# Two GpSimd drains among the last passes of a fused recurrence and mixture-of-experts kernel

## The chip, the cores and the metric

The kernel runs on one core of one Trainium2 chip. Its time is device microseconds of one launch, and the median of several runs counts. A core has five engines that run their own instruction queues: TensorE (PE in the profile; PEld is its weight load), VectorE (DVE), ScalarE (ACT), GpSimd (POOL) and SyncE (SP), which here issues transfers alone. They meet through semaphores.

## The reference

The first half is a gated linear recurrence over 768 steps in 4 x 8 heads of 48 channels; the second sends each of the 3072 resulting rows (8 heads x 48 = 384 wide) to one of 16 experts.

```python
f = 1.0 / (1.0 + np.exp(-f_logit))
for t in range(S):
    state = f[:, :, t, :, None] * state + np.einsum('bhd,bhe->bhde', k[:, :, t], v[:, :, t])
    y[:, :, t] = np.einsum('bhd,bhde->bhe', q[:, :, t], state)
# x: y with the heads of one step side by side, (3072, 384)
g_idx = argmax(x @ w_group);  e_idx = argmax(x @ w_expert[g_idx])
h = np.maximum(x[tok] @ w1[g, e], 0.0)            # (rows, 1024)
out[tok] = (g_w * e_w)[:, None] * (h @ w2[g, e])  # (rows, 384)
```

`g_w` and `e_w` are the softmax weights of the chosen group and expert.

## The kernel before, in words

The recurrence is computed in chunks of 128 steps with matmuls, and its rows are written to a table in DRAM, `x_dram`, each with its weight and its row number behind it. Along the way the kernel works out which rows each expert gets, ranks the experts by their number of rows, and fixes its passes. Two experts have 128 of their rows done in two early passes beside the recurrence (`early`, line 492). Then come sixteen passes, numbered 0 to 15, with one expert in each: the first and the last are 128 rows wide, and the fourteen between have widths from 230 down to 174 rows, listed in `WIDTHS`. What is beyond these widths would go through a loop behind a test at line 997 (`more > 0`); with these inputs that branch isn't taken.

The passes go through `for n in range(GE - 1)` (line 887) and a last part behind it. A pass does the following.

- `fetch` (line 390) gathers its rows from `x_dram` into the tile `xg`, one indirect transfer for each block of up to 128 rows. GpSimd issues it.
- The rows are turned so that the features lie on partitions (`square_in`, or `turn_in` for 128 rows).
- `up` (line 434) multiplies by the first weights, and `down` (line 467) by the second. A narrow pass (`down_rows`) has its result with the rows on partitions at once; a wide pass has it turned, in `yT`.
- The wide result is turned back: on VectorE in 32 x 32 squares (`square_out`, line 419), one turn of the loop later, or, for the last wide pass, on TensorE (`turn_out`, line 485).
- `put` (line 445) scales each row by its weight into a tile `yt`, of which there are four in turn, and GpSimd scatters it by row number to the output with an indirect transfer.

GpSimd computes nothing in this half. It issues the gathers three passes ahead and the scatters, two for each wide pass. The functions on the path of a scatter are `scaled` (line 480), which the loop calls for the pass before the current one, and `turn_out`, which the last part calls for the pass before the last.

The order of TensorE, VectorE, ScalarE and SyncE is written out by hand (`tc.manual_schedule`, line 85). GpSimd isn't in that list; its instructions are placed by the scheduler. The weights come on SyncE's queue, three passes ahead.

At the end of the program the compiler puts a closing part that the profile shows under line 1046: every engine drains, they meet at a barrier, the semaphores are cleared, and they meet once more. A drain is an instruction of an engine's queue behind which nothing of this queue starts until the engine has finished what was before it.

Of the kernel before, what the change touches and what calls it, by code (L numbers as in the profile page):

```python
# [1 line left out]

# [1 line left out]

# [13 lines left out]
ET = mybir.EngineType  # L18
P = 128
# [4 lines left out]
def kernel(  # L24
# [12 lines left out]
    nc = tc.nc  # L37
    B, H, S, D = q.shape
    N, DM = out.shape
# [3 lines left out]
    GE = G * EG  # L43
# [4 lines left out]
    KO = DM // P  # L48
# [28 lines left out]
    def const(shape, dtype, name):  # L77
        return cp.tile(shape, dtype, tag=name, name=name)

    def bank(shape, name):  # L80
        return ps.tile(shape, FP32, tag="bank", name=name)
# [9 lines left out]
    ident = const([P, P], FP32, "ident")  # L91
# [294 lines left out]
    def load_weights(pool, ap):  # L386
        e = value(ap, GE - 1)
        return load_layer(pool, e, 1), load_layer(pool, e, 2)

    def fetch(pool, rows, n, top=N, late=False):  # L390

        w = {"n": n, "pool": pool, "early": top < N, "late": late, "blocks": [(j, min(P, n - j * P)) for j in range((n + P - 1) // P)]}
        w["x"] = pool.tile([P, len(w["blocks"]), RW], FP32, tag="xg", bufs=2 if pool is ep else 6, name="xg")
        for j, m in w["blocks"]:
            nc.gpsimd.indirect_dma_start(out=w["x"][:, j, :], out_offset=None, in_=x_dram[0:1 + top, :], in_offset=bass.IndirectOffsetOnAxis(ap=rows[:, j:j + 1], axis=0))  # L395
        return w
# [15 lines left out]
    def square_in(w):  # L412

        w["xT"] = room(w, KO, "xe")
        x = w["x"][:, :, 0:DM].rearrange("p j (o g c) -> p j g o c", o=KO, c=SQ)
        xT = w["xT_full"].rearrange("p o (j k c) -> p j k o c", j=2, c=SQ)
        squares(w, lambda n, k_, rk, g, rg: nc.vector.transpose(out=xT[rg, 0:n, k_], in_=x[rk, 0:n, g]))  # L417

    def square_out(w):

        w["rows"] = w["pool"].tile([P, 2, DM], FP32, tag="yr", name="yr")
        y = w["rows"].rearrange("p j (o g c) -> p j g o c", o=KO, c=SQ)
        yT = w["yT_full"].rearrange("p o (j k c) -> p j k o c", j=2, c=SQ)
        squares(w, lambda n, k_, rk, g, rg: nc.vector.transpose(out=y[rk, 0:n, g], in_=yT[rg, 0:n, k_]))  # L424

    def turn_in(w):
        w["xT"] = room(w, KO, "xe")
        for j, m in w["blocks"]:
            pt = bank([P, KO, P], "xg_ps")
            for ko in range(KO):  # L430
                nc.tensor.transpose(out=pt[:, ko, 0:m], in_=w["x"][0:m, j, ko * P:(ko + 1) * P], identity=ident[0:m, 0:m])
            (nc.scalar.copy if w["early"] else nc.vector.tensor_copy)(w["xT"][:, :, j * P:j * P + m], pt[:, :, 0:m])
# [12 lines left out]
    def put(w, j, m, yp):  # L445

        y = w["pool"].tile([P, DM], FP32, tag="yt", bufs=2 if w["pool"] is ep else 4, name="yt")
        if w["n"] == P or "rows" in w:
            nc.scalar.activation(y[0:m], yp[0:m], AF.Copy, scale=w["x"][0:m, j, DM:DM + 1])  # L449
        else:  # L450
            nc.vector.tensor_scalar(y[0:m], yp[0:m], w["x"][0:m, j, DM:DM + 1], None, OP.mult)
        sent = nc.gpsimd.indirect_dma_start(out=out, out_offset=bass.IndirectOffsetOnAxis(ap=w["x"][0:m, j, DM + 1:RW].bitcast(U32), axis=0), in_=y[0:m], in_offset=None, bounds_check=N - 1, oob_is_err=False)  # L452
        if not w["late"]:

            tc.declare_no_dep(sent.ins, group="outputs", reason="each pass has rows of its own")
            tc.add_to_no_dep_group("outputs", sent.ins)
# [10 lines left out]
    def down(w, w2):  # L467
        n = w["n"]
        if n == P:
            for _ in down_rows(w, w2):  # L470
                pass
            return
        w["yT"] = w["yT_full"][:, :, 0:n]
        for m in range(KO):
            yp = bank([P, n], "yo")
            for fo in range(FO):
                nc.tensor.matmul(yp, lhsT=w2[:, fo, m * P:(m + 1) * P], rhs=w["h"][:, fo, :], start=(fo == 0), stop=(fo == FO - 1))  # L477
            nc.scalar.copy(w["yT"][:, m, :], yp)  # L478

    def scaled(w):  # L480
        if w["n"] > P:
            for j, m in w["blocks"]:
                put(w, j, m, w["rows"][:, j, :])

    def turn_out(w):
        for j, m in w["blocks"]:
            pt = bank([P, DM], "y_ps")
            for k_ in range(KO):
                nc.tensor.transpose(out=pt[0:m, k_ * P:(k_ + 1) * P], in_=w["yT"][:, k_, j * P:j * P + m], identity=ident)
            put(w, j, m, pt)  # L490

    def early():

# [342 lines left out]
    def pass_of(n):  # L836
        p = PLACES[n]
        if p < EARLY:
            return fetch(mo, rows_p[:, p, 1:2], P)
        return fetch(mo, rows_p[:, p, :], WIDTHS[p - EARLY])  # L840
# [3 lines left out]
    def weakest():  # L844

        worst = const([P, 1], FP32, "worst")
        nc.vector.tensor_reduce(out=worst, in_=decays.rearrange("p c a n -> p (c a n)"), axis=AX, op=OP.min)
        wt = bank([1, P], "wt")
        nc.tensor.transpose(out=wt, in_=worst, identity=ident)
        far = const([1, 2], FP32, "far")  # L850
        nc.vector.tensor_reduce(out=far[:, 0:1], in_=wt, axis=AX, op=OP.min)
        nc.vector.tensor_scalar(far[:, 1:2], far[:, 0:1], math.exp(-SAFE), None, OP.is_lt)
        nc.vector.tensor_copy(fari, far[:, 1:2])

    def flags():

        nc.vector.tensor_copy(both[:, 0:1], fari)
        nc.vector.tensor_scalar(rest, b_end, 0, None, OP.is_gt)
        nc.vector.tensor_tensor(both[:, 1:2], fari, rest, OP.max)
# [13 lines left out]
    def run_up(n):  # L873
        for _ in up(ws[n], ahead[n][0]):
            pass
# [11 lines left out]
    for n in range(GE - 1):  # L887
        w = ws[n]
        if n + 3 < GE:
            ws[n + 3] = pass_of(n + 3)  # L890
        if n == 0:
            ahead[2] = load_weights(wp, who[0:1, PLACES[2]:PLACES[2] + 1])
        past, coming = ws.pop(n - 1, None), ws.get(n + 2)
        if past and past["n"] > P:
            square_out(past)
        if coming and coming["n"] > P:
            square_in(coming)
        if n + 2 < GE:
            run_up(n + 1)
        if past:  # L900
            scaled(past)
        if coming and coming["n"] == P:
            turn_in(coming)
        w["yT_full"] = outs[n % 2]
        down(w, ahead.pop(n)[1])
        if n + 3 < GE:
            ahead[n + 3] = load_weights(wq if n % 3 == 1 else wp, who[0:1, PLACES[n + 3]:PLACES[n + 3] + 1])
        if n == 2:
            with tc.tile_pool(name="tb", bufs=1) as tb:
                beyond(False, tb)  # L910
        if n == 3:
            weakest()
            flags()


    last_up = up(ws[GE - 1], ahead[GE - 1][0])
    next(last_up)
    turn_out(ws.pop(GE - 2))
    for _ in last_up:
        pass  # L920
# [76 lines left out]
    with tc.If(more > 0), ExitStack() as late:  # L997
# [5 lines left out]
        with tc.For_i(0, last, 1) as i:  # L1003
# [14 lines left out]
            w = fetch(ep, row, P, late=True)  # L1018
# [32 lines left out]
```

## Time and profile before

| | |
|---|---|
| time, median of 3 runs | 430.03 us (428.63 to 430.20) |
| span of the profiled execution | 427.1 us |
| busy: TensorE, VectorE, ScalarE, GpSimd | 408.0, 267.1, 157.0, 83.1 us |
| transfers in all | 88.98 MB, 208 GB/s over the span |
| on GpSimd's queue (q0) | 5792 packets, 11.92 MB |
| scatters on GpSimd (line 452) | 32, 1076 ns each to issue |
| gathers on GpSimd (line 395) | 30 and 2, 987 and 1022 ns each to issue |
| the last scatter starts | 416.39 us |

The span runs from the program's first to its last instruction and is a little shorter than the time of a run. Busy time counts what an engine computes [...]. A drain or a semaphore step counts as no busy time, though it has a duration; it stands in the views of one source line, marked with a q behind the engine's name. The release of a wait is worked out from semaphore events.

### The profile page before, as it was taken

How to read it: one execution, taken by the hardware profiler on the slowest of the kernel's cores; microseconds unless marked ns; L12 is line 12 of the kernel's file. 1: busy time of each engine (PE TensorE's matmuls, PEld its weight loads, DVE VectorE, ACT ScalarE, POOL GpSimd, SP SyncE). 2: the span in 40 equal slices, each digit the busy share in tenths (PEclk: the TensorE clock that was granted, in tenths of full speed). 3: DMA queues.
4: the chain of work that ended last, by engine and by line, in shares of the span. 5: the costliest groups of instructions: out<-in, count | busy, mean ns of one | idle time of the engine just before them, and what ended most of it. 6: DMA issues, size and time to landing. Idle time of an engine off the chain costs nothing.

```text
span 427.1 us, 10087 instructions
## 1 busy us (share of the span) xinstructions
PE 408.0 (96%) x4067; PEld 382.7 (90%) x4067; DVE 267.1 (63%) x778; ACT 157.0 (37%) x341; POOL 83.1 (19%) x127
## 2 busy tenths in 40 slices
PE   4999999999999999999999999999999999999990
PEld 2888989999889978989999999999999999999960
DVE  5665686868798741640899759468568559553410
ACT  5667666666664411211212123123123123123210
POOL 4000010101012047001042122221321321022120
PEclk9999999999999999999999999999999999999996
DMA  9999999999999639975828549569478569544010
GB/s 166 176 181 185 185 161 181 153 151 152 202 344 401 244 119 355 385 280 189 286 74 316 186 185 326 162 235 315 136 268 278 183 260 329 177 168 161 20 40 15
DMA packets 132121, 88.98 MB, mean 208 GB/s; under 512 B 102630, under 2 KB 122700, under 8 KB 132066
## 3 DMA queue, kind: packets, MB, share of 16 engines
q1 hardware_dynamic: 125666, 75.50, 65.8%
q0 software_dynamic: 5792, 11.92, 9.2%
q8 instruction: 34, 0.56, 0.6%
q10 hardware_dynamic: 608, 0.83, 0.6%
q14 instruction: 21, 0.17, 0.1%
HBM read 78.71 MB, written 9.83 MB: 207 GB/s over the span
## 4 chain that ended last, share of the span: by engine, by line
PE 49%; issue 30%; DMA 9%; POOL 6%; DVE 2%; ACT 2%; POOLq 0%; DVEq 0%
PE hp L441 12%; PE yo L477 6%; DMA out_dram<-yt,xg 6%; PE ap L645 4%; PE y L689 4%; POOL out_dram L452 4%; PE cs L585 4%; PE yo L462 4%; PE x_ps L729 3%; PE lT L704 2%; POOL xg L395 2%; PE tr_q L619 2%; DMA ends<-eq 2%; PE tr_k L619 2%; PE y L684 2%
## 5 line engine op out<-in xcount | busy, mean ns | idle before, releaser
L441 PE MATMUL hp<-xe,w 128*128 128x128 f32 (+14 forms) x864 | 138.6, 320 | 0.0
L441 PEld LDWEIGHTS hp<-xe,w 128*128 128x128 f32 x864 | 135.8, 190 | 0.8
L477 PE MATMUL yo<-h,w 128*128 128x230 f32 (+13 forms) x672 | 115.8, 333 | 0.0
L424 DVE STREAM_TRANSPOSE yr<-yT 32x192 f32<-32x192 f32 (+1 forms) x208 | 70.5, 339 | 70.4 <-ACT yT L478 67.8
L477 PEld LDWEIGHTS yo<-h,w 128*128 128x128 f32 x672 | 113.7, 190 | 0.2
L417 DVE STREAM_TRANSPOSE xe<-xg 32x192 f32<-32x192 f32 (+1 forms) x208 | 69.7, 335 | 8.6 <-PE hp L441 5.6
L442 ACT ACTIVATE h<-hp 128x256 f32<-128x256 f32 (+14 forms) x72 | 34.4, 478 | 103.6 <-PE hp L441 103.6
L452 POOL DMA_INDIRECT out_dram<-yt,xg x32 | 34.4, 1076 | 150.6 <-ACT yt L449 145.0
L478 ACT COPY yT<-yo 128x230 f32<-128x230 f32 (+13 forms) x42 | 13.5, 326 | 80.5 <-PE yo L477 80.5
L648 DVE TENSOR_TENSOR am<-ap,tri 128x512 f32<-128x512 f32 x48 | 29.8, 682 | 17.0 <-PE ap L645 16.9
L395 POOL DMA_INDIRECT xg<-x_dram,rows_p x30 | 29.6, 987 | 51.3 <-DMA out_dram<-yt,xg 27.5
L585 PE MATMUL cs<-ld_f,tri 128*128 128x384 f32 x48 | 19.5, 531 | 5.5 <-ACT ld_f L579 5.5
L645 PE MATMUL ap<-Tq,Tk 48*64 48x128 f32 x768 | 23.8, 272 | 0.2 <-ACT Tk L620 0.2
L689 PE MATMUL y<-am,v 128*64 128x128 f32 x384 | 23.3, 273 | 0.0
L645 PEld LDWEIGHTS ap<-Tq,Tk 48*64 48x64 f32 x768 | 20.8, 133 | 2.0 <-issue 1.1
L689 PEld LDWEIGHTS y<-am,v 128*64 128x64 f32 x384 | 21.5, 137 | 0.6 <-DVE am L648 0.5
L462 PE MATMUL yo<-w,h 128*128 128x384 f32 x64 | 21.3, 486 | 0.0
L462 PEld LDWEIGHTS yo<-w,h 128*128 128x128 f32 x64 | 11.9, 190 | 7.4
L585 PEld LDWEIGHTS cs<-ld_f,tri 128*128 128x128 f32 x48 | 8.5, 200 | 9.8 <-POOL blank L170 5.2
L592 POOL DMA_DIRECT2D ends<-eq x10 | 5.4, 541 | 60.3 <-ACT eq L586 60.3
L449 ACT ACTIVATE yt<-yr,xg 128x384 f32<-128x384 f32 (+13 forms) x26 | 14.4, 604 | 5.4 <-DVE yr L424 5.4
L692 ACT COPY xT<-y 128x512 f32<-128x512 f32 x24 | 12.9, 589 | 9.3 <-PE y L689 9.3
(170 smaller groups left out, 385.0 us busy)
## 6 DMA issues: line engine op xcount, KB each, us to landing
w<-in_moe_w_dram SPq DMA_DIRECT2D x34, 1536.0 KB, 10.2
qh<-in_q_dram SPq DMA_DIRECT2D x12, 384.0 KB, 6.8
ld_k<-in_k_dram SPq DMA_DIRECT2D x12, 384.0 KB, 6.5
v<-in_v_dram SPq DMA_DIRECT2D x12, 384.0 KB, 7.3
ld_f<-in_f_logit_dram SPq DMA_DIRECT2D x11, 384.0 KB, 6.6
x_dram<-x_kept SPq DMA_DIRECT2D x2, 1536.0 KB, 12.0
x_dram<-x POOLq DMA_DIRECT2D x2, 384.0 KB, 7.9
x_dram<-x ACTq DMA_DIRECT2D x2, 384.0 KB, 7.5
```

Of the source, the lines that this page charges most:

```text
L395: nc.gpsimd.indirect_dma_start(out=w["x"][:, j, :], out_offset=None, in_=x_dram[0:1 + top, :], in_offset=bass.IndirectOffsetOnAxis(ap=rows ...
L417: squares(w, lambda n, k_, rk, g, rg: nc.vector.transpose(out=xT[rg, 0:n, k_], in_=x[rk, 0:n, g]))
L424: squares(w, lambda n, k_, rk, g, rg: nc.vector.transpose(out=y[rk, 0:n, g], in_=yT[rg, 0:n, k_]))
L441: nc.tensor.matmul(hp[:, o, :], lhsT=w1[:, ko, (f + o) * P:(f + o + 1) * P], rhs=w["xT"][:, ko, :], start=(ko == 0), stop=(ko == KO - 1))
L442: nc.scalar.activation(h[:, f:f + 2, :], hp, AF.Relu)
L452: sent = nc.gpsimd.indirect_dma_start(out=out, out_offset=bass.IndirectOffsetOnAxis(ap=w["x"][0:m, j, DM + 1:RW].bitcast(U32), axis=0), in ...
L462: nc.tensor.matmul(yp, lhsT=w["h"][:, fo, :], rhs=w2[:, fo, :], start=(fo == 0), stop=(fo == FO - 1))
L477: nc.tensor.matmul(yp, lhsT=w2[:, fo, m * P:(m + 1) * P], rhs=w["h"][:, fo, :], start=(fo == 0), stop=(fo == FO - 1))
L585: nc.tensor.matmul(cs.rearrange("t h d -> t (h d)"), lhsT=tri, rhs=nl[:, b], start=True, stop=True)
L645: nc.tensor.matmul(ap[r][half, a, :], lhsT=w["Tk"][rows, b, a, half], rhs=w["Tq"][rows, b, a, :], start=True, stop=True)
L648: nc.vector.tensor_tensor(am[:, r], ap[r], tri.unsqueeze(1).broadcast_to((P, HP, P)), OP.mult)
L689: nc.tensor.matmul(ys[r][DP * b:DP * b + DP, a, :], lhsT=w["v"][:, b, 2 * a + r, :], rhs=w["am"][b][:, r, a, :], start=(c == 0 and a == 0) ...
```

## The change

Two drains are put into GpSimd's queue. The first comes behind the second scatter of pass 12 (the pass before the loop's current one when `n == GE - 3`), the second behind the second scatter of pass 14, which `turn_out` makes. A context manager `settled` does it: where it is switched on, GpSimd's instructions in its body keep their written order, and a `drain` follows them. It is on for a block `j` above 0, so for the second of two blocks alone. What they are for: GpSimd is to be done with the transfers it has issued so far at these two places, rather than at the end of the program.

```diff
-    def scaled(w):
+    def scaled(w, settle=False):
         if w["n"] > P:
             for j, m in w["blocks"]:
-                put(w, j, m, w["rows"][:, j, :])
+                with settled(settle and j):
+                    put(w, j, m, w["rows"][:, j, :])
+
+    @contextmanager
+    def settled(on):
+
+        with ExitStack() as turn:
+            if on:
+                turn.enter_context(tc.manual_schedule(engines={ET.Pool}))
+            yield
+            if on:
+                nc.gpsimd.drain()
 
     def turn_out(w):
         for j, m in w["blocks"]:
-            pt = bank([P, DM], "y_ps")
-            ...
-            put(w, j, m, pt)
+            with settled(j):
+                turn_out_block(w, j, m)
+
+    def turn_out_block(w, j, m):
+        pt = bank([P, DM], "y_ps")
+        ...
+        put(w, j, m, pt)
...
         if past:
-            scaled(past)
+
+            scaled(past, n == GE - 3)
```

No other instruction is added or taken away, and the order of the others is the same on each engine.

More of the change, by code (lines that the diff above doesn't have):

```diff
@@ L1 @@
-from contextlib import ExitStack
+from contextlib import ExitStack, contextmanager
 import math
@@ L478, in down @@
             nc.scalar.copy(w["yT"][:, m, :], yp)
-    def scaled(w):
+    def scaled(w, settle=False):
         if w["n"] > P:
             for j, m in w["blocks"]:
-                put(w, j, m, w["rows"][:, j, :])
+                with settled(settle and j):
[8 more added lines that the diff above has]
+                nc.gpsimd.drain()
     def turn_out(w):
         for j, m in w["blocks"]:
-            pt = bank([P, DM], "y_ps")
-            for k_ in range(KO):
-                nc.tensor.transpose(out=pt[0:m, k_ * P:(k_ + 1) * P], in_=w["yT"][:, k_, j * P:j * P + m], identity=ident)
-            put(w, j, m, pt)
+            with settled(j):
+                turn_out_block(w, j, m)
+    def turn_out_block(w, j, m):
+        pt = bank([P, DM], "y_ps")
+        for k_ in range(KO):
+            nc.tensor.transpose(out=pt[0:m, k_ * P:(k_ + 1) * P], in_=w["yT"][:, k_, j * P:j * P + m], identity=ident)
+        put(w, j, m, pt)
     def early():
```

## The prediction

> **What bounds the kernel now.** I read the whole page first, then the end of the span by windows, then GpSimd's own queue in order of time, and last the two lines of the program that hold its opening and its closing.
>
> The page says that the kernel is TensorE's for nearly all of its length: matmuls cover 96% of the span, and their row of tenths falls only in the last slice. The change touches no TensorE, VectorE or ScalarE instruction, so it can pay only where TensorE isn't at work: at the end.
>
> ```profile
> span 427.1 us, 10087 instructions
> PE 408.0 (96%) x4067; PEld 382.7 (90%) x4067; DVE 267.1 (63%) x778; ACT 157.0 (37%) x341; POOL 83.1 (19%) x127
> PE   4999999999999999999999999999999999999990
> DMA  9999999999999639975828549569478569544010
> ```
>
> The windows of the last 34 us are the view that carries the forecast. Columns: the window, its length, busy us (and instructions) of PE, PEld, DVE, ACT, POOL, then the clock and the DMA share and rate.
>
> ```profile
> 393.30:403.70 10.40, 10.40 (x72) 10.40 (x71) 5.12 (x16) 1.29 (x4) 0.01 (x1) 1.00 0.04 9
> 403.70:409.40 5.70, 5.70 (x52) 5.68 (x52) 1.13 (x2) 2.19 (x7) 4.12 (x4) 1.00 0.22 83
> 409.40:416.20 6.80, 6.05 (x24) 3.58 (x23) 0.00 (x0) 0.97 (x2) 0.00 (x0) 1.00 0.06 15
> 416.20:419.20 3.00, 0.00 (x0) 0.00 (x0) 0.00 (x0) 0.00 (x0) 0.99 (x1) 0.96 0.13 51
> 419.20:427.10 7.90, 0.00 (x0) 0.00 (x0) 0.00 (x0) 0.00 (x0) 0.00 (x0) 0.50 0.00 1
> ```
>
> In the last 7.9 us no engine computes and the DMA share is 0.00. What fills them is seen in the program's closing line (1046), GpSimd's part and SyncE's part of it; the opening line (1037) gives a drain that has nothing to drain. Columns: shortest/median/longest in ns, then first and last start in us.
>
> ```profile
> L1046 POOLq DRAIN  x3: 46/103/6767, 419.2 to 426.8; - x3
> L1046 POOLq EVENT_SEMAPHORE  x4: 17/17/17, 426.3 to 427.0; - x4
> ...
> L1046 SPq DRAIN  x3: 7/7/13, 419.9 to 426.6; - x3
> ...
> L1037 POOLq DRAIN  x1: 184/184/184, 0.3 to 0.3; - x1
> ```
>
> The first of GpSimd's three closing drains is the 6767 ns one (the next GpSimd record on the line, a semaphore step, comes at 426.3, and 419.2 + 6.77 is 426.0). All others wait for it: SyncE starts its own closing drains at 419.9, is at the barrier by 420.0, and sits there. So 6.8 us of the span are one GpSimd instruction on the path that sets the end.
>
> What does it drain? The last scatter starts at 416.39 and lands 2.5 us later, at 418.9, before this drain starts; so it waits for no data. It is bookkeeping, and the candidates for what it counts are the transfers that GpSimd has issued. Its queue near the end (start us, duration us, instruction, and in brackets the idle time before it):
>
> ```profile
> 390.74 1.00 POOL L452 DMA_INDIRECT out_dram<-yt,xg  x1 [11.63 <-ACT yt L449]
> 392.05 1.26 POOL L452 DMA_INDIRECT out_dram<-yt,xg  x1 [0.30 <-issue]
> 403.92 0.99 POOL L452 DMA_INDIRECT out_dram<-yt,xg  x1 [10.61 <-ACT yt L449]
> 405.21 0.96 POOL L452 DMA_INDIRECT out_dram<-yt,xg  x1 [0.30 <-issue]
> 406.88 1.00 POOL L452 DMA_INDIRECT out_dram<-yt,xg  x1 [0.71 <-DVE yt L451]
> 408.18 1.18 POOL L452 DMA_INDIRECT out_dram<-yt,xg  x1 [0.30 <-issue]
> 416.39 0.99 POOL L452 DMA_INDIRECT out_dram<-yt,xg  x1 [7.04 <-ACT yt L449]
> ```
>
> Between these pairs it idles 10.6 and 7.0 us. The issue counts are 32 scatters, 30 + 2 gathers, 10 of ends, 6 of meta and 2 of x: 82 transfers.
>
> **What the skill says.** The Trainium skill, "VectorE: DVE Perf Modes", section "The DRAIN you can't avoid", puts the drains of a program's opening and closing at about 12 ns on all engines. The trace agrees for four engines (SyncE 7 to 13 ns) and contradicts it for GpSimd: 46, 103, 184 and 6767 ns. "Perfetto Trace Analysis", section "Sequencer-only Instruction (DRAIN, etc)", says that the profiler shows execution alone for such an instruction and not its semaphore wait; so 6.77 us would be the drain's own work, which fits the landing above. "DMA: Bandwidth & Descriptors", section "SWDGE vs HWDGE vs iDMA", says that two GpSimd cores write a pair of descriptors per operation into rings in SBUF. That makes a ledger that grows with each transfer plausible, but no page states what a GpSimd drain costs. "PSUM — Partial Sum Buffer", section "Engine vs sequencer instructions", says a drain waits for the engine to go fully idle; whether that takes in transfers in flight no run here shows yet, so I price both readings.
>
> **The change part by part.** The only new instructions are two GpSimd drains: one after the second scatter of pass 12 (392.05), one after the second of pass 14 (408.18). The order hints around them leave every instruction on all five engines in its old order, so they cost nothing; splitting the function that turns rows out costs nothing for the same reason.
>
> *Price of a drain.* A bare one takes 46, 103 or 184 ns; I take 0.11 us, about their mean. If the rest of the last drain is shared by the 82 transfers, each costs (6.77 - 0.11) / 82 = 0.081 us. That is my estimate from this trace; the trace holds no second loaded drain to test it. The bounds: 0 per transfer (all 6.77 fixed), or 0.081 per transfer.
>
> *Drain 1* has 82 - 5 = 77 transfers behind it: 0.11 + 77 x 0.081 = 6.3 us. Scatter 392.05 has been issued by 393.31 and lands 5.5 us after its start, at 397.5. If the drain works through the finished ones while the last flies, it ends near 399.6; if it first waits for the landing and then counts, at 397.5 + 6.3 = 403.8. Behind it on GpSimd stand the four scatters of passes 13 and 14, the first of which starts at 403.92. So it fits into the idle 10.6 us either way. TensorE is busy throughout (10.40 of 10.40) and waits for no scatter, since no gather remains after 352 us and the four yt buffers leave ScalarE and VectorE four scatters of room. Even a drain that ends 2 us late only shifts four back-to-back scatters whose next successor is at 416.39. Cost on the path: 0. VectorE's transposes run in 397.6 to 403; a shared port could stretch the drain, and that same room takes it up.
>
> *Drain 2* has four new transfers: 0.11 + 4 x 0.081 = 0.43 us. The scatter at 408.18 lands 4.2 us later, at 412.4; the drain ends at 412.8 at the latest. Behind it stands the last scatter (416.39), for which the end waits; 3.6 us are spare. Cost: 0.
>
> *The closing drain* then has one transfer left: 0.11 + 0.08 = 0.19 us instead of 6.77. It would end at 419.2 + 0.19 = 419.4, and then it isn't the last any more: SyncE arrives at 420.0. So the barrier is met at about 420.0 instead of 426.3, and the gain is 426.3 - 420.0 = 6.3 us, not 6.6. The two later drains and the semaphore clearing (426.5 to 427.1) stay.
>
> Sum: 430.03 - 6.3 = 423.7 us, 1.5% less.
>
> **The rivals.**
>
> *A fixed drain, hidden.* The 6.77 us do not depend on the count: a queue that was ever used costs that much. For: four drains, three bare and one loaded, fit a step as well as a slope. Against: nothing was in flight, and a fixed 6.77 us beside 46 to 184 ns needs some cause other than the transfers. The closing drain stays; drain 2 runs 409.4 to 416.1 beside the landing, before 416.39: 430.0 us.
>
> *A fixed drain, or one that counts all transfers from the first each time, after the landing.* As above, but drain 2 starts its 6.77 us only at 412.4 and ends at 419.1; the last scatter slips from 416.39 by 2.8 us, and the closing drain follows in full: 432.8 us, 0.65% slower. For: two drains could then only add. Against: work that each drain repeats in full leaves nothing finished by it.
>
> *Half fixed.* If half of the 6.77 us is fixed, the closing drain still takes 3.4 us: the barrier at 419.2 + 3.4 + 0.3 = 422.9 (0.3 us being the step from the drain's end, 426.0, to the semaphore's 426.3), a gain of 3.4 us: 426.6 us. Drain 2 ends by 412.4 + 3.6 = 416.0, just in time.
>
> **How the numbers follow.** I give the count 0.82, half fixed 0.06, fixed and hidden 0.06, after the landing 0.06. The bound of 0.5% is 2.15 us: faster means under 427.9, so both of the first go there, with a little of the half-fixed case lost to a larger share: 0.87. Same 0.07, slower 0.06. The runs before spread from 428.63 to 430.20; less 6.3 that is 422.3 to 423.9. The low end takes 0.3 more for a closing drain and semaphore step that shrink with the ledger: 422.0. The high end takes in the half-fixed case and its spread: 427.2. Outside lie the two fixed cases, 0.12.
>
> **What would show it.** Right: in the changed trace, a GpSimd drain of 4 to 10 us from 393.3 which ends before 404; a second of 0.4 to 3.5 us from 409.4; a first closing drain under 0.6 us; the span shorter by about 6 us, with TensorE's busy time, the matmul order and the time of the last scatter (416.4) unchanged. Wrong: a closing drain that still takes several us, or a last scatter later than 416.4, which would show drain 2 in its way; or a first new drain that is short while the last stays long, which would mean that a drain in the middle doesn't do what the last one does.

## The result and the profile after

The changed kernel takes 422.75 us (median of 4 runs, 421.97 to 423.67) beside 429.42 us for the kernel before in the same runs (428.63 to 430.20). The ratio is 0.9845, interval 0.9811 to 0.9880: 6.7 us or 1.55% faster. The forecast was 423.7 us with a gain of 6.3 us.

The page of the changed kernel, its first line and the matmul row of tenths:

```profile
span 420.2 us, 10089 instructions
PE 408.4 (97%) x4067; PEld 383.3 (91%) x4067; DVE 267.1 (64%) x778; ACT 156.7 (37%) x341; POOL 83.2 (20%) x127
PE   4999999999999999999999999999999999999995
```

Two instructions more, the same busy times, and the span ends with matmuls in half of its last slice. GpSimd's queue in order of time, changed kernel. The columns are the start and the duration in us of the instruction that issues a transfer (this issuing is what counts as GpSimd's busy time here), the instruction, and the idle time before it:

```profile
390.55 1.00 POOL L452 DMA_INDIRECT out_dram<-yt,xg  x1 [11.63 <-ACT yt L449]
391.86 1.26 POOL L452 DMA_INDIRECT out_dram<-yt,xg  x1 [0.30 <-issue]
403.73 0.99 POOL L452 DMA_INDIRECT out_dram<-yt,xg  x1 [10.61 <-ACT yt L449]
405.03 0.96 POOL L452 DMA_INDIRECT out_dram<-yt,xg  x1 [0.30 <-issue]
406.69 1.00 POOL L452 DMA_INDIRECT out_dram<-yt,xg  x1 [0.71 <-DVE yt L451]
407.99 1.18 POOL L452 DMA_INDIRECT out_dram<-yt,xg  x1 [0.30 <-issue]
416.20 0.99 POOL L452 DMA_INDIRECT out_dram<-yt,xg  x1 [7.04 <-ACT yt L449]
```

Every scatter has kept its place: all starts are 0.18 to 0.19 us earlier than before, and the idle times are the same to 0.01 us. No scatter waits for a drain. GpSimd's drains and its counter step, by source line (shortest/median/longest ns, first and last start us); line 494 is the change's own, 1013 is the test before the branch that isn't taken (997 before), 1062 is the closing part (1046 before):

```profile
L494 POOLq DRAIN  x2: 5178/7388/9597, 391.0 to 407.2; - x2
L1013 POOLq INC_SWDGE_SEM  x1: 205/205/205, 417.5 to 417.5; - x1
L1062 POOLq DRAIN  x3: 46/102/1070, 417.7 to 419.9; - x3
```

and the same counter step in the kernel before:

```profile
L997 POOLq INC_SWDGE_SEM  x1: 1842/1842/1842, 417.4 to 417.4; - x1
```

The closing drain went from 6767 to 1070 ns, short as forecast, though not as short as the 0.19 us of the forecast. A second instruction shrank with it: the counter step (INC_SWDGE_SEM in the profile, at the line of the branch that isn't taken) went from 1842 to 205 ns. The forecast's sum doesn't hold it; its range left 0.3 us for a semaphore step that shrinks. The two are one stretch of GpSimd's path: counter step, drain, barrier. The last window, changed kernel, in the columns of the prediction:

```profile
416.20:420.20 4.00, 0.00 (x0) 0.00 (x0) 0.00 (x0) 0.00 (x0) 0.99 (x1) 0.95 0.10 40
```

After the start of the last scatter 4.0 us remain; it was 10.7 us (427.1 - 416.4).

### The profile page after: what moved, and what is told of

Read it like the earlier page. It is cut to its first block, busy times and chain, and to the rows that moved or that the text cites. A ratio compares the mean times of both kernels' runs of the same rounds, so it can differ in the third digit from the quotient of the medians.

```text
span 420.2 us, 10089 instructions
## 1 busy us (share of the span) xinstructions
PE 408.4 (97%) x4067; PEld 383.3 (91%) x4067; DVE 267.1 (64%) x778; ACT 156.7 (37%) x341; POOL 83.2 (20%) x127
## 3 DMA queue, kind: packets, MB, share of 16 engines
q0 software_dynamic: 5792, 11.92, 9.5%
## 4 chain that ended last, share of the span: by engine, by line
PE 53%; issue 29%; DMA 8%; POOL 6%; ACT 1%; POOLq 1%; DVE 1%; SPq 0%
PE hp L441 12%; PE yo L477 6%; DMA out_dram<-yt,xg 6%; PE ap L660 5%; PE y L704 5%; PE cs L600 4%; PE yo L462 4%; POOL out_dram L452 4%; PE x_ps L744 3%; PE lT L719 3%; PE tr_q L634 3%; POOL xg L395 2%; PE tr_k L634 2%; PE y L699 2%; PE ds L677 2%
## 5 line engine op out<-in xcount | busy, mean ns | idle before, releaser
L395 POOL DMA_INDIRECT xg<-x_dram,rows_p x30 | 29.6, 987 | 51.5 <-DMA out_dram<-yt,xg 27.4
```

## The experiments

A number that doesn't move with the start of a run is the tail: from the end of the last matmul (start plus duration of its row in the timeline) to the end of the span. The row of the changed kernel is

```profile
409.93 5.33 PE L462 MATMUL yo<-w,h 128*128 128x384 f32 x16
```

so its tail is 420.17 - 415.26 = 4.9 us, and that of the kernel before 427.12 - 415.45 = 11.7 us. The kernels were timed in three sets beside the kernel before, which took 429.1, 435.4 and 429.3 us in them; ratios are to the kernel before of the same set.

**The changed kernel again**, no edit.

> The changed kernel once more, beside the two kernels with one drain each, so that the three stand on one chip. Every theory: about 6.7 us under the kernel before; closing drain about 1.1 us, which is mostly the landing of the last scatter.

423.48 us, ratio 0.9864 (0.9827 to 0.9901); closing drain 1247 ns, tail 5.1 us. Its last scatter landed 2.7 us after its start instead of 2.5.

**Only the first drain.**

```diff
     def turn_out(w):
         for j, m in w["blocks"]:
-            with settled(j):
+            with settled(False):
```

> Only the drain behind pass 12; five transfers are left to the closing drain. Count theory (0.11 us + 0.081 us for each transfer since the last drain): 0.5 us of work, which fits beside the last landing, so the time is that of the changed kernel within 0.3 us. Rival, a drain settles only what was in flight at it: the closing drain stays near 6.8 us and the time near that of the kernel before.

422.61 us, ratio 0.9845 (0.9817 to 0.9873), tail 4.9 us. Five transfers were left; the counter step and the closing drain:

```profile
L1013 POOLq INC_SWDGE_SEM  x1: 302/302/302, 417.8 to 417.8; - x1
L1062 POOLq DRAIN  x3: 46/102/1133, 418.4 to 420.5; - x3
```

The last scatter lands at 419.28 and the drain ends at 419.52, so nearly all of its 1133 ns is that landing. The second drain of the change brings nothing that these runs can tell. The rival, that a drain settles only what is in flight, falls: the other 77 didn't come back.

**Only the second drain.**

```diff
-            scaled(past, n == GE - 3)
+            scaled(past)
```

> Only the drain behind pass 14, with 81 transfers before it (6.7 us of work by the count). Work beside the landing: the drain ends near 416, just before the last scatter at 416.2, and the time is that of the changed kernel within 0.5 us. Work after the landing (412.2): the drain ends near 418.9, the last scatter slips by 2.7 us, and so does the time. Fixed cost: the same lateness, and a closing drain of 6.8 us on top.

424.06 us, ratio 0.9884 (0.9856 to 0.9913), tail 5.4 us. The new drain and the last scatter in its own queue:

```profile
L494 POOLq DRAIN  x1: 8703/8703/8703, 407.3 to 407.3; - x1
```
```profile
416.90 1.00 POOL L452 DMA_INDIRECT out_dram<-yt,xg  x1 [7.57 <-ACTq L1013]
```

The scatter before the drain is issued by 409.33 and lands at 412.29; the drain ends at 416.02, which is 6.7 us after the issue and not 6.7 us after the landing. So at least a part of the work runs beside the landing. It is just too late: the last scatter starts 1.47 us after the last matmul (415.43) instead of 0.94, and 0.5 us is lost. The profile names ScalarE for this wait, but the scatter starts 0.88 us behind the drain's end, as one does behind the drain after pass 13 below (412.91 to 413.79), whose rows had long been ready.

**One drain earlier, so that more is left.** The first edit leaves 20 transfers to the close, the second 36; the second drain is off in both, as above.

```diff
-            scaled(past, n == GE - 3)
+            scaled(past, n == GE - 8)
```
```diff
-            scaled(past, n == GE - 3)
+            scaled(past, n == GE - 12)
```

> One drain, behind pass 7; 20 transfers are left. Count theory: closing drain 0.11 + 20 x 0.081 = 1.7 us, and about 1 us more time than the changed kernel. A fixed cost: about 1 us or 6.8 us, not between.

> One drain, behind pass 3; 36 transfers are left. Count theory: closing drain 0.11 + 36 x 0.081 = 3.0 us. A cost by packets: scatters and gathers carry nearly all packets, so the same within 0.3 us. A fixed cost: about 1 us or 6.8 us.

The counter step and the closing drain with 20 left, then with 36 left:

```profile
L1013 POOLq INC_SWDGE_SEM  x1: 602/602/602, 419.8 to 419.8; - x1
L1062 POOLq DRAIN  x3: 46/103/1831, 420.8 to 423.1; - x3
```
```profile
L1013 POOLq INC_SWDGE_SEM  x1: 922/922/922, 424.0 to 424.0; - x1
L1062 POOLq DRAIN  x3: 46/103/3137, 425.3 to 429.0; - x3
```

With the 6767 and 1842 ns of the kernel before, these are three points of a line: (3137 - 1831) / 16 = 82 ns and (6767 - 3137) / 46 = 79 ns for each transfer, and a rest of 1831 - 20 x 80 = 0.24 us. For the counter step it is (922 - 602) / 16 = 20 ns and (1842 - 922) / 46 = 20 ns, and a rest of 602 - 20 x 20 = 202 ns; the 302 ns with five left lie on the same line, and the 205 ns with one left 17 ns under it.

The count is of transfers and not of packets. The 82, 36 and 20 transfers hold 5792, 2816 and 1776 packets, about 65 for each transfer down to 20 left and 89 for each of these, so the two slopes alone can't tell the two apart. The rest can: at (3137 - 1831) / 1040 = 1.26 ns for each packet the last 20 would take 2.2 us, and the drain took 1.83. The counter step says it more sharply, as with five left (384 packets) a cost by packets would give 0.17 us and 302 ns were seen. The 46 transfers between 36 and 82 hold 18 plain ones (16 of 4 KB and two of 384 KB) beside 28 gathers and scatters, the other 36 are gathers and scatters alone, and both kinds cost the same.

Their times, of one run each, are 425.28 us (first set) and 431.12 us (second set); the tails are 5.5 and 7.1 us.

**Forty small transfers more**, without drains and with the two of the change. They were meant for ten passes, but the scheduler issued all of them at the start, from 4.6 to 30.5 us.

```diff
+    spare = dp.tile([40, D + 2], FP32, name="spare")
...
+        if 2 <= n < 12:
+            for i in range(4):
+                nc.gpsimd.dma_start(out=spare[4 * (n - 2) + i:4 * (n - 2) + i + 1, :], in_=blank)
```

> No drain of its own, and 40 more GpSimd transfers of one row of 200 bytes each, to a spare place in DRAM, spread over ten passes: 122 transfers. Cost by transfer: closing drain 0.11 + 122 x 0.081 = 10.0 us. Cost by packets or bytes (the 40 add under a tenth of the 5792 packets): 6.8 to 7.4 us. Cost fixed: 6.8 us.

> The same 40 more transfers, with the two drains of the change: 117 transfers before the first one. Cost by transfer: the first drain is about 3.2 us longer than the changed kernel's 9.6 us and ends near 404, at the next scatter; the closing drain stays near 1.1 us, so the time is that of the changed kernel within 0.5 us, apart from what the 40 issues cost on the way. Cost by packets: the first drain stays near 9.6 us.

Both missed. (The forty also brought 1280 packets, 22% of the 5792 and not under a tenth.) Without drains the closing drain is not 10.0 us, and not 6.8 either:

```profile
L1018 POOLq INC_SWDGE_SEM  x1: 471/471/471, 430.8 to 430.8; - x1
L1067 POOLq DRAIN  x3: 46/103/1971, 431.3 to 433.9; - x3
```

The counter step says (471 - 202) / 20 = 13 or 14 transfers left of 122; so about 108 were settled with no drain. The queue of this kernel shows where:

```profile
403.90 1.00 POOL L452 DMA_INDIRECT out_dram<-yt,xg  x1 [11.62 <-ACT yt L449]
407.23 1.27 POOL L452 DMA_INDIRECT out_dram<-yt,xg  x1 [2.33 <-issue]
```

Between these two, the 116th and 117th transfer, stand 2.33 us for which the profile finds no cause; the same pair, the scatters of pass 12, has 0.30 in the kernels before and after. The kernel with drains has the same 2.33 us, and its first drain, right behind this pair, then ends only about 0.4 us after the landing before it (estimated from the last packet of that scatter), where the changed kernel's first drain ends 3.2 us after it: little was left to settle. The times are 435.99 us without drains (one run) and 435.14 us with them, ratio 0.9985 (0.9961 to 1.0009). I can't set this against the forty transfers' own price: the tails are 5.6 us without drains and 5.4 with them, so the closing is short in both, and TensorE's busy time in the first 150 us is 138 and 139 us where two other kernels of the same set (the drain behind pass 3 and the one behind every pass) have 142.

**Twenty small transfers more**, no drain, to stay below that point: the same edit with two for each turn.

```diff
-            for i in range(4):
+            for i in range(2):
```

> No drain of its own, and 20 more transfers of 200 bytes at the start: 102 in all, fewer than the 116 at which the run with forty more cleared its own books. From the closing drains with 82, 36 and 20 transfers left (0.24 us + 0.080 us each) and the counter step before it (0.185 us + 0.020 us each). Cost by transfer: closing drain 8.4 us, counter step 2.25 us. Cost by packets (each small transfer brought 32 packets in the run with forty more, against 5792 for the 82): closing drain 7.5 us, counter step 2.0 us.

Missed again, and in the same way: a short counter step, a short closing drain, and a gap of its own in GpSimd's queue, now before the 101st transfer.

```profile
L1018 POOLq INC_SWDGE_SEM  x1: 400/400/400, 419.5 to 419.5; - x1
L1067 POOLq DRAIN  x3: 46/102/1769, 419.9 to 422.6; - x3
```
```profile
408.73 1.00 POOL L452 DMA_INDIRECT out_dram<-yt,xg  x1 [0.70 <-DVE yt L451]
411.74 1.18 POOL L452 DMA_INDIRECT out_dram<-yt,xg  x1 [2.02 <-issue]
```

(400 - 202) / 20 = 10 were left of 102, so 92 had been settled in 2.02 - 0.30 = 1.7 us; in the run with forty more it was about 108 in 2.0 us: 19 ns each both times. That the work is done in the gap is inferred from this, and from the short drain right behind the gap above; no view shows it. Its one run took 424.66 us beside 429.25 before, with no drain at all; its tail is 5.6 us. The point isn't a number of transfers: with twenty small ones fewer it came after four more scatters. Nor is it a number of packets: 6512 had gone ahead of the one gap, 6224 ahead of the other.

**A drain behind every wide pass.**

```diff
-            scaled(past, n == GE - 3)
+            scaled(past, True)
```

> A drain behind the second scatter of every wide pass. Count theory: nothing more than the changed kernel, since little is left to the end there either; the time within 0.3 us of it. Rival, a drain that holds a gather: the gathers of the middle passes stand behind the drains, start 2 to 5 us later, and the time rises by 1 us or more.

429.33 us beside 435.42, ratio 0.9868 (0.9841 to 0.9895); tail 5.3 us. The interval is too wide for the 1 us of the rival, but the trace answers it for TensorE. The 14 drains start between 220.5 and 415.1 us, and over that stretch TensorE is busy throughout (columns of the prediction's windows, from 176 us on):

```profile
176.00:421.00 245.00, 245.00 (x1432) 239.89 (x1430) 150.00 (x442) 56.97 (x129) 50.77 (x48) 0.99 0.59 209
```

TensorE does wait in this kernel, before the matmuls of a first expert layer:

```profile
PE hp L441 <- issue: 2.3, 5, 0.7
```

But these waits lie at 171 to 175 us, ahead of the first drain, and the kernel with one drain behind pass 3, of the same set, has such waits there too, also ahead of its drain. So a drain behind every pass costs the matmuls nothing here. It is a mild test of a held gather, though: the idle time ahead of the gathers is 61.2 us in all where it is 58.9 in the changed kernel. In the changed kernel they wait nearly as long for other things, the landing of scatters above all (27.4 us), and with the drains no gather starts over 1.7 us later behind the scatter ahead of it than without.

**One drain in the way of scatters**, behind pass 13, with the second drain off as above.

```diff
-            scaled(past, n == GE - 3)
+            scaled(past, n == GE - 2)
```

> One drain, behind the second scatter of pass 13, with 79 transfers before it: 0.24 + 79 x 0.080 = 6.6 us beside the landing, until about 412.6. It lies in the way of the two scatters of pass 14, which were issued at 406.7 and 408.0: they start at about 412.7 and 414.0. If the reserve before the last scatter is what counts, the last scatter keeps its place behind the last matmul and the time is that of the changed kernel within 0.5 us. If a drain in the way of scatters costs its lateness, the time is 5 to 6 us longer than that.

423.78 us, ratio 0.9869 (0.9835 to 0.9903): the same ratio as the repeated changed kernel, though with an interval of 1.5 us to either side, and far from the 5 to 6 us of the rival. Its queue and its counter step, with three left:

```profile
405.42 0.96 POOL L452 DMA_INDIRECT out_dram<-yt,xg  x1 [0.30 <-issue]
413.79 0.99 POOL L452 DMA_INDIRECT out_dram<-yt,xg  x1 [7.41 <-issue]
415.09 1.17 POOL L452 DMA_INDIRECT out_dram<-yt,xg  x1 [0.30 <-issue]
416.60 0.99 POOL L452 DMA_INDIRECT out_dram<-yt,xg  x1 [0.34 <-ACT yt L449]
```
```profile
L1013 POOLq INC_SWDGE_SEM  x1: 262/262/262, 417.6 to 417.6; - x1
```

The drain holds the two scatters of pass 14 by some 7 us, and the last scatter starts 0.94 us behind the last matmul as always. What it does cost is in the landing: the three scatters now fly together, the last lands after 3.6 us instead of 2.5, and the tail is 6.1 us, some 1 us more than the changed kernel's, which the times of whole runs are too coarse to show.

## Why the prediction was right

*The closing drain is bookkeeping by transfers.* Right, and shown: 82, 36 and 20 left give one line. The prediction had 0.11 us + 0.081 us each; the line has 0.24 + 0.080. The fixed-cost rivals and the half-fixed case are out, and so is a drain that repeats what an earlier one did.

*Drain 1 is free.* Right. The record starts at 391.0, before the scatter ahead of it (391.86), so it takes in more than the drain's own work. The prediction read such a record as the drain's work alone, which held for the closing drain before, as that one starts after the last landing. It ends at 400.56, between the two ends that were given (399.6 beside the landing, 403.8 after it). Neither reading is exact: half of the work can run beside the landing, and half comes behind it. Where a drain outlasts the last landing before it, the stretch behind the landing is 0.08, 0.16, 0.24 and 3.20 us with 1, 3, 5 and 77 transfers (closing drains of the changed kernel, of the drain behind pass 13 and of the first drain alone; first drain of the change, 400.56 - 397.36). That is 0.04 us for each transfer and 0.04 to 0.12 besides, about half of the whole price. Where the landing comes early, the whole counts from the end of the issue: behind pass 13 with 79 it is 406.38 + 0.24 + 79 x 0.080 = 412.9 (seen 412.9). A pair of lists would do that; the Trainium skill, "DMA: Bandwidth & Descriptors", section "SWDGE vs HWDGE vs iDMA", has a read and a write descriptor for each operation, but no run here looks into the drain: the halves are in the times, and what they are stays open.

*Drain 2 is free.* Right, it ends at 412.3. That it is also needless was not seen: without it the closing drain, with five transfers left, ends 0.24 us after the last landing instead of 0.08, still before SyncE is at the barrier (419.5 against 420.0).

*A late drain only shifts scatters.* Right to the microsecond that the landing costs (drain behind pass 13).

*The gain is 6.3 us, since SyncE's arrival at 420.0 takes over.* The mechanism is right, the size off by 0.6 us in the spans (427.1 - 420.2 = 6.9, of which 0.2 is an earlier end of the matmuls). The mis-sized term is SyncE's arrival, which the sum took as fixed. SyncE's semaphore waits and drains in the closing part, before and then changed:

```profile
L1046 SPq EVENT_SEMAPHORE  x14: 17/28/28, 419.2 to 427.1; - x14
```
```profile
L1062 SPq EVENT_SEMAPHORE  x14: 17/28/957, 417.6 to 420.1; - x14
L1062 SPq DRAIN  x3: 7/7/13, 419.3 to 419.6; - x3
```

SyncE's first wait ends with the counter step (419.2 before, 417.7 changed), and the kernels with one drain behind pass 7 and behind pass 3 bear it out: their counter steps end at 420.45 and 424.97, and SyncE's first record is at 420.40 and 424.92. (In the kernel with twenty transfers more it comes only with the last landing, at 421.30.) The step costs 20 ns for each unsettled transfer, so it fell from 1842 to 205 ns. SyncE began at 417.6 instead of 419.2, waited 957 ns for the last landing (418.7), and reached the barrier at 419.4 instead of 420.0. It is now the last to come, 0.6 us behind the end of the closing drain (418.8). The price of a transfer at the close, as long as GpSimd is the last at the barrier, is 80 + 20 = 100 ns, not 81.

*What would show it.* Two of the signs were set too narrowly: the second drain took 5.2 us of record (forecast 0.4 to 3.5) and the closing one 1.07 us (forecast under 0.6). Both records start earlier than assumed and hold the landing of the scatter before them.

## What to carry to other kernels

Look at what stands behind the last compute instruction: here it was a drain of 6.8 us that no busy time counts. If GpSimd has issued many transfers, one drain in a gap of its queue takes that work off the end; in this kernel it took 0.24 us + 0.08 us for each transfer since the last drain, and more where a landing came late, and the next transfer started 0.88 us behind its end (416.02 to 416.90 with only the second drain, 412.91 to 413.79 behind pass 13). All of that has to fit ahead of the next transfer that the end waits for, and one drain was enough. Don't place it right before the last scatter (the second drain alone lost 0.5 us), nor so that held scatters fly together with the last one (1.1 us of landing).

## What the runs showed of the hardware

A drain on GpSimd has a price by transfers issued since the last one, 0.24 us + 0.080 us each (20, 36 and 82 left), and a counter step at a branch that isn't taken has one of 202 + 20 ns each (3, 5, 20, 36 and 82 left).

GpSimd also settles its transfers on its own once it has issued enough of them: about 108 in 2.0 us before the 117th and 92 in 1.7 us before the 101st transfer, 19 ns each against 80 ns in a drain. The closing drain is then short without any drain in the kernel (1.97 and 1.77 us, landing of the last scatter included), and the kernel with twenty useless transfers more was quicker than the kernel before (424.66 us beside 429.25, one run). The kernel before, with 82 transfers, ended without such a gap and paid for all of them at the close. What sets the point stays open. That twenty small transfers stood for four scatters rules out a fixed number of transfers; room in some list would be a guess, and no run tried a kernel with more scatters alone.
